# A fused attention and two-expert-layer kernel: the first two dense steps as plain products, sums of token quarters spread over the second, another order of loads and of the last routed block

## Chip, cores and metric

One core of a Trainium2 chip runs the whole kernel in one launch. The metric is the device time of a run in microseconds (us); lower is better.

## What is computed

Three layers in float32, cut here to what matters:

```
x = attention(rotate(q), rotate(k), v)              # 2 x 8 heads, 576 tokens, 64 wide -> x (1152, 512)
# layer 1: each token goes to one of 8 experts
out[e's tokens] = gate * (relu(x[e's tokens] @ w1[e]) @ w2[e])      # w1 (8,512,1024), w2 (8,1024,512)
# layer 2: all tokens go through all 8 experts, weighted by P
P = exp(x @ w_gate - max); 8 times: P /= row sums; P /= column sums; P *= N / E
out = sum over e of P[:, e:e+1] * (relu(x @ w1[e]) @ w2[e])
```

## The kernel before, in words

The matrix products take float32 operands as a high part (float32r) and a low part, the rest: A·B is A_hi·B_hi + A_hi·B_lo + A_lo·B_hi, three passes. ACT rounds the high part (a copy to float32r), DVE subtracts it to get the low part. TensorE (PE) is the engine that all of this feeds.

**Routed part.** Tokens are sorted into blocks of 128 that belong to one expert; `run_blocks` walks over 14 of them (two more sit in a branch that is taken only if the routing needs them). A block's first product is `block_l1` (line 645), its second `block_l2` (672): 8 pieces k of 128 rows, for each the passes hi·hi, hi·lo, lo·hi, all into one PSUM bank. The second weight matrix comes in two halves, each split into `whi` by ACT (L623) and `wlo` by DVE (L616). `block_out` scales the result on ACT (L685) and scatters it to `yd` in DRAM by an indirect DMA of POOL's queue (L686). Beside the blocks, `next(dense)` (L768) moves the generator `dense_experts` on, which loads and splits the first weights of the dense part (blocks 4 to 12).

**Dense part.** All 1152 tokens go through 8 experts in 32 steps of 256 hidden units (`STEPS`). A step's first product is done in the way of Strassen and Winograd: seven products (`l1`, L1086, 12 matmuls of 288 columns each) of sums of quarters of the tokens with sums of quarters of the weights, where plain multiplication takes eight. Quarters 1 to 4 of the tokens and the sums 5, 6, 7 and 4 lie in `yq`, high and low parts apart (index `YQ`). The weights' sums are made by `prep1` in five parts. A step's second product, nine token tiles of six 512-column matmuls (`l2`, L1138), trails by one step: in the loop over n the tiles are of step n - 1. In the first step ACT copies their results to `acc` (L1142); later DVE adds them (L1144, L1149). The tiles go through two PSUM banks ("o"), which the small matmuls of `sinkhorn` (the rounds that make P) use as well.

**The handover.** `yd` is read back in four quarters of 288 tokens (`g`, 576 KB each, 96 partitions with 3 rows of 512, L973). `turn_quarter` (976) transposes a quarter on PE, after as many idle products (L982) as its second argument says, which keep TensorE busy while the load runs; `split_quarter` (989) makes the high and low parts. The first step is done by `plain` (1092) in four calls of 24 matmuls: two terms a, two halves k, three passes, two column halves q. The second step (n = 1 of the loop) already takes the seven products, and the sums of quarters are made as it goes (`sums`, 1004): a DVE operation over 1152 columns (L1007, L1009, L1011), then a split on ACT (L954) and DVE (L955).

Inside `manual_schedule` the order of the code is the order on PE, DVE, ACT and POOL; SP's DMA queue follows its own waits.

Of the kernel before, what the change touches and what calls it, by code (L numbers as in the profile page):

```python
# [10 lines left out]
F32 = mybir.dt.float32  # L11
# [19 lines left out]
NS = 14  # L31
KD_, KF = DM // 128, F // 128
TQ, QW = 96, 288
# [14 lines left out]
def fused_kernel(ctx, tc, qk, vv, tab, cst, emb, tau, w1a, w2a, wg, w1b, w2b, out):  # L48
# [23 lines left out]
    idx = keep.tile([BLK, 2, NB], U32, name="idx")  # L72
    bei = keep.tile([1, NB + 1], I32, name="bei")

    def fetch(raws, src, n, e, cond=None, only=range(4)):
# [436 lines left out]
    with tc.manual_schedule(engines=ORDERED | {mybir.EngineType.SP}):  # L512
# [4 lines left out]
        for k in range(len(units) + LAG):  # L517
# [6 lines left out]
            if 20 < k < 60 and k % 10 in (7, 8):  # L524

                m, x = divmod(2 * (k // 10 - 2) + k % 10 - 7, 4)
                fetch((raw1, raw2)[m], (w1a, w2a)[m], (128, 256)[m], 0, only=(x,))
            if out_rows is not None:
# [142 lines left out]

    def block_l2(h, w, between=None):
        p = bank("y", 2, "y")
        for k in range(KF):
            if k == KF // 2 and between:
                between()
            kk = slice(k * 128, (k + 1) * 128)
            wk = [w[k // 2][x][:, (k % 2) * 512:(k % 2 + 1) * 512] for x in range(2)]
            for n, (a, b) in enumerate(((h[0], wk[0]), (h[0], wk[1]), (h[1], wk[0]))):
                T.matmul(p, a[:, kk], b, start=(k == 0 and n == 0), stop=(k == KF - 1 and n == 2))  # L680
        return p
# [13 lines left out]
    def run_blocks(lo, hi, xb=None, w1=None, w2=None):  # L695
# [11 lines left out]
        with tc.manual_schedule(engines=ORDERED):  # L707
# [10 lines left out]
            for i in range(lo, hi + 1):  # L718
# [32 lines left out]
                if i > lo:  # L751

                    turned = []
                    y = block_l2(h, w2, (lambda: turned.append(block_turn(hn))) if i == hi - 1 else None)
                if i == 1:
# [6 lines left out]
                if here:  # L762
# [3 lines left out]
                    h = turned[0] if i == hi - 1 else block_turn(hn)  # L766
                if NS - 10 <= i < NS - 1:
                    next(dense)  # L768

    reg = [0]  # L770
    with tc.manual_schedule(engines=ORDERED | {mybir.EngineType.SP}):
# [15 lines left out]
        banks(mctx, "pm")  # L787
        dense = dense_experts(ctx, tc, yd, wg, w1b, w2b, out, ident, ones)
        run_blocks(0, NS, xb, pieces(first_w1), first_w2)
# [8 lines left out]

def dense_experts(ctx, tc, yd, wg, w1b, w2b, out, ident, ones):

# [71 lines left out]

    def prep_first():

        for f in range(2):
            yield
            w1[0, f] = wtile(4)
            wsplit(w1[0, f], raw1[0][:, :, f])
        fetch1(2)

# [39 lines left out]
    yield  # L920
    yield from prep_first()
    for part in (0, 1, 1.5, 2, 3):
        yield
        prep1(1, part)
    yield
# [35 lines left out]
    G.memset(wgt, 0.0)  # L961
    nc.sync.dma_start(out=wgt[:, :, :E], in_=wg.rearrange("(k p) e -> p k e", p=128))

# [39 lines left out]

    def sums(p):

# [4 lines left out]
        elif p == 4:  # L1010
            V.tensor_tensor(b21, b21, b22, op=ALU.subtract)  # L1011
        split_sum(p, {5: t1, 6: b22, 7: b11, 4: b21}[p])

# [77 lines left out]

    def plain(r, c):

        d = take()
        w = w1[0, r]
# [3 lines left out]
        for i, (a, y, k, wx, yx) in enumerate(todo):  # L1099
            for q in range(2):  # L1100
                T.matmul(d[1][:, q, :QW], wv[:, wx, a, k], yq[yx][:, y, k, q * QW:(q + 1) * QW],  # L1101
# [51 lines left out]
    with tc.manual_schedule(engines=ORDERED):  # L1153

        hs[0] = htile()
        d = [turn_quarter(0, 40), turn_quarter(1, 0)]
        split_quarter(0, d[0])
        d.append(turn_quarter(2, 6))
        split_quarter(1, d[1])
        c11 = plain(0, 0)  # L1160
        split_quarter(2, d[2])
        d.append(turn_quarter(3, 0))
        c21 = plain(1, 0)
        parts(0, 11, c11)
# [3 lines left out]
        next(sk)  # L1168
        c12 = plain(0, 1)
        parts(0, 21, c21)  # L1170
        sums(6)
        for n in range(2):
            fetch2(n)
        c22 = plain(1, 1)
        parts(0, 12, c12)
        sums(5)
        prep2(0)
        parts(0, 22, c22)
        for n in range(1, STEPS + 1):
            second, last = n == 1, n == STEPS  # L1180

# [24 lines left out]
            do(parts, n, 11)  # L1206
            if second:
                sums(7)
            weights(0)
# [4 lines left out]
            product(5)  # L1214
            if second:
                sums(4)
            tile_(3)
# [75 lines left out]
```

## Time and profile before

| | |
|---|---|
| Runs | 1173.98, 1176.97, 1178.61 us; median 1176.97 |
| The profiled execution | 1175.93 us, span on the core 1174.1 us |
| PE busy | 1134.9 us, 97% of the span |
| DVE, ACT, POOL busy | 833.1, 510.0, 135.0 us |
| Dense matmuls L1086 | 2604 of 288 columns, 381.1 us |
| Dense matmuls L1138 | 1728 of 512 columns, 434.3 us |

Times in the profile count from the span's start. Attention comes first, the routed blocks run to 381 us, the handover to 399.5 us, and the dense steps from there to the end. "Idle before" names what released an engine. Matmuls are pipelined, so their rows overlap and their spacing is shorter than their length.

### The profile page before, as it was taken

The numbers are of one execution on the slowest core, as the hardware profiler recorded it, in microseconds if no ns is written. First come the engines' busy times: TensorE is split into PE (matmuls) and PEld (weight loads), VectorE is DVE, ScalarE is ACT, GpSimd is POOL, SyncE is SP. The second block draws the span as 40 slices with busy tenths as digits, with TensorE's granted clock in tenths as the row PEclk, the third lists the DMA queues.
The fourth block names the chain that finished last, engine by engine and source line by source line (L and its number), as shares of the span: only waits on it lengthen the run. The fifth ranks groups of instructions, "written<-read, shape, count | busy, mean of one in ns | idle before, by whom it ended". The sixth has DMA issues, their size and how long they took to land.

```text
span 1174.1 us, 17220 instructions
## 1 busy us (share of the span) xinstructions
PE 1134.9 (97%) x6698; PEld 970.9 (83%) x6700; DVE 833.1 (71%) x1284; ACT 510.0 (43%) x775; POOL 135.0 (11%) x95
## 2 busy tenths in 40 slices
PE   8798997999999979999999999999999999999998
PEld 3576775788887768999989998999899999989997
DVE  6876766988996368776766676667666766676665
ACT  3555654788986343333333333233323332333230
POOL 4646402134231000000000000000000000000000
PEclk9999998999999999999999999999999999999999
DMA  7478623347285501111111111111111111111002
GB/s 231 115 222 238 181 59 111 127 150 254 69 299 207 127 19 55 54 36 37 54 54 37 36 54 55 37 36 55 53 39 36 54 50 42 37 51 48 29 1 80
DMA packets 74882, 103.63 MB, mean 88 GB/s; under 512 B 5288, under 2 KB 45224, under 8 KB 73904
## 3 DMA queue, kind: packets, MB, share of 16 engines
q1 hardware_dynamic: 71792, 93.54, 26.3%
q0 software_dynamic: 2432, 7.93, 1.9%
q8 instruction: 53, 0.87, 0.3%
q10 hardware_dynamic: 576, 1.05, 0.2%
q14 instruction: 29, 0.24, 0.1%
HBM read 111.09 MB, written 8.39 MB: 102 GB/s over the span
## 4 chain that ended last, share of the span: by engine, by line
PE 63%; DVE 2%; DMA 1%; issue 1%; ACT 1%; SPq 0%; POOLq 0%; ACTq 0%
PE o L1138 33%; PE d L1086 28%; DMA g<-yd 1%; PE d L1101 1%; DMA yd<-y,idx 0%; DVE yq L955 0%; PE o L1030 0%; PE d L985 0%; DVE w L853 0%; DVE h L1126 0%; PE d L982 0%; ACT yq L954 0%; DVE w L915 0%; ACT h L1125 0%; DVE yt L1007 0%
## 5 line engine op out<-in xcount | busy, mean ns | idle before, releaser
L1138 PE MATMUL o<-w,h 128*128 128x512 f32 x1728 | 434.3, 393 | 4.8 <-ACT acc L1142 4.2
L1086 PEld LDWEIGHTS d<-yq,w 128*128 128x128 f32 x2604 | 368.3, 188 | 18.8
L1086 PE MATMUL d<-yq,w 128*128 128x288 f32 x2604 | 381.1, 295 | 0.0
L1138 PEld LDWEIGHTS o<-w,h 128*128 128x128 f32 x1728 | 312.6, 188 | 60.5 <-ACT acc L1142 5.1
L1149 DVE SCALAR_TENSOR_TENSOR acc<-o,P,acc 128x512 f32<-128x512 f32 x252 | 189.2, 751 | 159.6 <-PE o L1138 159.6
L1125 ACT ACTIVATE h<-st 128x576 fp32r<-128x576 f32 x93 | 63.7, 685 | 218.6 <-DVE st L1115 218.5
L1112 ACT ACTIVATE st<-d 128x576 f32<-128x576 f32 x93 | 60.8, 653 | 220.0 <-PE d L1086 220.0
L616 DVE TENSOR_TENSOR wlo<-raw,whi 128x2048 fp32r<-128x2048 f32 x56 | 127.9, 2289 | 14.0 <-ACT whi L623 14.0
L623 ACT ACTIVATE whi<-raw 128x2048 fp32r<-128x2048 f32 x52 | 99.9, 1920 | 8.8 <-DVE n L116 4.0
L1115 DVE TENSOR_TENSOR st<-st,d 128x576 f32<-128x576 f32 x93 | 69.9, 751 | 40.7 <-PE d L1086 40.7
L235 DVE TENSOR_REDUCE nb<-s 120x1 f32<-120x576 f32 (+1 forms) x80 | 60.2, 753 | 36.7 <-PE s L229 26.4
L241 ACT ACTIVATE p<-s,nb 120x576 f32<-120x576 f32 (+1 forms) x80 | 59.1, 738 | 58.2 <-DVE nb L235 56.6
L852 ACT ACTIVATE w<-raw 128x512 fp32r<-128x512 f32 x126 | 72.3, 574 | 19.9 <-DVE raw L898 15.3
L853 DVE TENSOR_TENSOR w<-raw,w 128x512 fp32r<-128x512 f32 x126 | 77.9, 619 | 0.1
L1126 DVE SCALAR_TENSOR_TENSOR h<-st,h 128x576 fp32r<-128x576 f32 x93 | 69.8, 751 | 2.5 <-ACT h L1125 2.4
L229 PE MATMUL s<-kd,qd 128*120 128x288 f32 x280 | 55.7, 322 | 6.0 <-DMA qd<-hl 3.1
L229 PEld LDWEIGHTS s<-kd,qd 128*120 128x120 f32 x280 | 39.5, 183 | 19.6 <-issue 8.2
L282 PE MATMUL o<-ph,vr 120*64 120x288 f32 x320 | 48.1, 421 | 0.0
L680 PE MATMUL y<-wlo,hh 128*128 128x512 f32 x112 | 43.8, 391 | 1.8 <-DVE wlo L616 1.8
L680 PE MATMUL y<-whi,hh 128*128 128x512 f32 x112 | 45.0, 402 | 0.0
L269 DVE COPY ph<-pt 120x480 f32<-120x480 f32 x64 | 41.3, 647 | 2.0 <-PE pt L263 1.7
L686 POOL DMA_INDIRECT yd<-y,idx x14 | 26.5, 1893 | 126.6 <-ACT y L685 96.6
(256 smaller groups left out, 1142.0 us busy)
## 6 DMA issues: line engine op xcount, KB each, us to landing
raw<-w1a SPq DMA_DIRECT2D x56, 512.0 KB
raw<-w2a SPq DMA_DIRECT2D x56, 512.0 KB
raw<-w1b SPq DMA_DIRECT2D x64, 256.0 KB
raw<-w2b SPq DMA_DIRECT2D x32, 512.0 KB
r<-qk SPq DMA_DIRECT2D x7, 1152.0 KB
kd<-hl SPq DMA_DIRECT2D x28, 288.0 KB
qd<-hl SPq DMA_DIRECT2D x24, 144.0 KB
g<-yd SPq DMA_DIRECT2D x4, 576.0 KB
```

Of the source, the lines that this page charges most:

```text
L229: T.matmul(s[:m, h, :HS], qd[:, j, t * QT:t * QT + m], kd[:, j, x, h * HS:(h + 1) * HS], start=(x == 0), stop=(x == 1))
L616: V.tensor_tensor(lo, raw, hi, op=ALU.subtract)
L623: A.activation(hi, raw, AF.Copy)
L680: T.matmul(p, a[:, kk], b, start=(k == 0 and n == 0), stop=(k == KF - 1 and n == 2))
L852: A.activation(hi, src, Copy)
L853: V.tensor_tensor(lo, src, hi, op=ALU.subtract)
L1086: T.matmul(d[1][:, q, :QW], wv[:, wx, which, k], yq[yx][:, YQ[p], k, q * QW:(q + 1) * QW], start=new and k == 0 and (wx, yx) == (0, 0), st ...
L1115: V.tensor_tensor(halves(st[x]), halves(st[x]), mid(d), op=ALU.add)
L1125: A.activation(hi, src, AF.Relu)
L1126: V.scalar_tensor_tensor(lo, src, 0.0, hi, op0=ALU.max, op1=ALU.subtract)
L1138: T.matmul(d, hs[n][:, r, hx, t * 128:(t + 1) * 128], w2[n][:, wx, r], start=(r == 0 and (hx, wx) == (0, 0)), stop=(r == 1 and hx == 1))
L1149: V.scalar_tensor_tensor(a, d, p, a, op0=ALU.mult, op1=ALU.add)
```

## The change

- `block_l2` gets an order for the last block alone (`high_first`): in each half of the pieces the passes with the weights' high part come first, eight of them, and the four with the low part behind. In the order of code this is block 13's second product; blocks 0 to 12 keep theirs.
- The dense weights of steps 0 and 1 are both prepared plain (`prep_plain`): two splits each, without sums. The generator has six stages in place of nine and starts at block 7 in place of 4.
- The gate weights `wg` are loaded during attention (after unit 72) into a small tile `wgk`, and POOL copies them to `wgt`; the load between the first two quarter loads goes.
- A quarter's load puts tokens 3p, 3p+1, 3p+2 into partition p, one piece of 1536 elements; the transposes then write each third column of the bank.
- Idle products: 34 ahead of the first quarter, 6 ahead of the second, none ahead of the third (before: 40, 0, 6).
- Step 1 is done by `plain` as well, in four calls of 24 matmuls. Between them stand the tiles of step 0, the rounds of `sinkhorn` (two for each of the last three calls), and the sums: `split_sums` of one sum, then `add_up` of the next, which is split one call later. The loop begins at n = 2.

```
-    def block_l2(h, w, between=None):
+    def block_l2(h, w, between=None, high_first=False):
...
+        todo = [(k, a, b) for k in range(KF) for a, b in ((0, 0), (0, 1), (1, 0))]
+        if high_first:
+            todo.sort(key=lambda x: (x[0] // (KF // 2), x[2]))
...
-                if NS - 10 <= i < NS - 1:
+                if NS - 7 <= i < NS - 1:
                     next(dense)
...
-    yield from prep_first()
-    for part in (0, 1, 1.5, 2, 3):
-        yield
-        prep1(1, part)
+    for n in range(2):
+        yield from prep_plain(n)
...
-    nc.sync.dma_start(out=wgt[:, :, :E], in_=wg.rearrange("(k p) e -> p k e", p=128))
+    G.tensor_copy(wgt[:, :, :E], wgk)
...
-        nc.sync.dma_start(out=g, in_=yd[i * QW:(i + 1) * QW].rearrange("(t p) d -> p t d", p=TQ))
+        nc.sync.dma_start(out=g, in_=yd[i * QW:(i + 1) * QW].rearrange("(p t) d -> p t d", t=3))
...
-                T.transpose(bank(d[k // 2], k % 2)[:, t * TQ:(t + 1) * TQ], gs[i][:, t, k * 128:(k + 1) * 128],
+                T.transpose(bank(d[k // 2], k % 2)[:, t:QW:3], gs[i][:, t, k * 128:(k + 1) * 128],
...
-        d = [turn_quarter(0, 40), turn_quarter(1, 0)]
+        d = [turn_quarter(0, 34), turn_quarter(1, 6)]
         split_quarter(0, d[0])
-        d.append(turn_quarter(2, 6))
+        d.append(turn_quarter(2, 0))
...
+        c = plain(1, 0, 0, between(0, 0))
         parts(0, 22, c22)
-        for n in range(1, STEPS + 1):
+        split_sums(5)
+        add_up(6)
+        l2(0, 1)
+        parts(1, 11, c)
+        c = plain(1, 1, 0, between(2, 1))
+        split_sums(6)
+        add_up(7)
+        l2(0, 3)
+        parts(1, 21, c)
+        prep1(2, 0)
+        c = plain(1, 0, 1, between(4, 2))
+        split_sums(7)
+        add_up(4)
+        l2(0, 5)
+        prep2(1)
+        parts(1, 12, c)
+        prep1(2, 1)
+        prep1(2, 1.5)
+        c = plain(1, 1, 1, between(6, 3))
+        prep1(2, 2)
+        l2(0, 7)
+        parts(1, 22, c)
+        split_sums(4)
+        prep1(2, 3)
+        l2(0, 8)
+        for n in range(2, STEPS + 1):
```

How the order moves at three places. First PE at the handover (`d` and `o` are PSUM banks, `w` the first dense weights, `io` the identity, `g` the token quarters). Before:

```order
L982 MATMUL d<-w 128x512 x40
L985 MATMUL d<-io,g 128x96 x18
L985 MATMUL o<-io,g 128x96 x6
L982 MATMUL d<-w 128x512 x6
L985 MATMUL d<-io,g 128x96 x12
L1101 MATMUL d<-yq_4045,w 128x288 x2
```

and now:

```order
L985 MATMUL d<-w 128x512 x34
L988 MATMUL d<-io,g 128x96 x12
L985 MATMUL d<-w 128x512 x6
L988 MATMUL d<-io,g 128x96 x6
L988 MATMUL o<-io,g 128x96 x6
L988 MATMUL d<-io,g 128x96 x12
L1108 MATMUL d<-yq_4037,w 128x288 x2
```

The six idle products moved from behind the second quarter's transposes to ahead of them. Second, SP's queue at the same place, before:

```order
L80 DMA raw_77<-w2a 128x2x512
L790 UNCONDITIONAL_BRANCH x2
L973 DMA g<-yd 96x3x512
L962 DMA lw<-wg 128x4x8
L973 DMA g<-yd 96x3x512 x3
L871 DMA raw_4308<-w2b 128x2x512
```

and now:

```order
L81 DMA raw_78<-w2a 128x2x512
L795 UNCONDITIONAL_BRANCH x2
L976 DMA g<-yd 96x1536 x4
L876 DMA raw_4291<-w2b 128x2x512
L876 DMA raw_4293<-w2b 128x2x512
```

The load of `wg` is gone from between the first and the second quarter. Third, DVE in the second dense step (`yt` holds the sums, `yq` their parts, `h` the hidden units' low part), before:

```order
L1115 TENSOR_TENSOR st<-st,d 128x576
L1126 SCALAR_TENSOR_TENSOR h<-st,h 128x576
L1009 TENSOR_TENSOR yt<-yt 128x1152
L955 TENSOR_TENSOR yq_4046<-yt,yq_4045 128x1152
L853 TENSOR_TENSOR w<-raw_3097,w 128x512
L891 TENSOR_TENSOR raw_3097<-raw_3097 128x2x128
```

and now:

```order
L958 TENSOR_TENSOR yq_4038<-yt,yq_4037 128x1152
L1012 TENSOR_TENSOR yt<-yt 128x1152
L1133 SCALAR_TENSOR_TENSOR h<-d,h 128x576
L858 TENSOR_TENSOR w<-raw_3444,w 128x512
L896 TENSOR_TENSOR raw_3444<-raw_3444 128x2x128
L958 TENSOR_TENSOR yq_4038<-yt,yq_4037 128x1152
L1014 TENSOR_TENSOR yt<-yt 128x1152
```

Before, a sum (`yt<-yt`) was split at once (`yq<-yt`); now a split is followed by the next sum, and three other operations stand between that and its split.

## Rows read from the trace of the kernel before

**Rows 1.** Page, part 1: busy time of each engine, share of the span, instructions.
```profile
PE 1134.9 (97%) x6698; PEld 970.9 (83%) x6700; DVE 833.1 (71%) x1284; ACT 510.0 (43%) x775; POOL 135.0 (11%) x95
```

**Rows 2.** Stages: length, busy us of PE, PEld, DVE, ACT, POOL, clock, DMA share, GB/s.
```profile
290.00:373.00 83.00, 83.00 (x407) 69.27 (x406) 74.13 (x57) 69.97 (x66) 24.31 (x12) 1.00 0.57 203
373.00:382.00 9.00, 6.50 (x27) 4.54 (x25) 4.59 (x2) 3.48 (x4) 1.92 (x1) 1.00 0.08 33
382.00:399.50 17.50, 15.56 (x82) 12.80 (x83) 4.30 (x8) 4.22 (x9) 1.18 (x2) 0.90 0.77 176
399.50:416.20 16.70, 16.70 (x163) 15.66 (x162) 8.69 (x13) 8.00 (x15) 0.00 (x0) 1.00 0.11 38
416.20:449.10 32.90, 26.78 (x152) 22.82 (x151) 24.12 (x56) 15.81 (x26) 0.00 (x0) 1.00 0.11 34
449.10:474.60 25.50, 24.89 (x149) 22.26 (x148) 22.27 (x61) 8.27 (x14) 0.00 (x0) 1.00 0.19 57
474.60:498.20 23.60, 23.60 (x139) 21.28 (x139) 15.81 (x26) 7.71 (x12) 0.00 (x0) 1.00 0.17 50
```

**Rows 3.** Timeline of the last routed block: start us, length us, engine, line, op.
```profile
373.44 2.29 DVE L616 TENSOR_TENSOR wlo<-raw,whi 128x2048 fp32r<-128x2048 f32 x1 [1.01 <-ACT whi L623]
...
373.48 0.47 PE L680 MATMUL y<-whi,hh 128*128 128x512 f32 x1
...
375.78 0.50 PE L680 MATMUL y<-wlo,hh 128*128 128x512 f32 x1 [1.83 <-DVE wlo L616]
...
376.21 2.29 DVE L616 TENSOR_TENSOR wlo<-raw,whi 128x2048 fp32r<-128x2048 f32 x1 [0.48 <-ACT whi L623]
...
378.63 0.42 PE L680 MATMUL y<-wlo,hh 128*128 128x512 f32 x1
...
380.94 0.39 PE L680 MATMUL y<-whi,hl__3720 128*128 128x512 f32 x1
381.42 0.69 ACT L685 ACTIVATE y<-y,gate 128x512 f32<-128x512 f32 x1 [5.25 <-issue]
```

**Rows 4.** Timeline of the handover, same columns.
```profile
382.21 9.37 PE L982 MATMUL d<-w 128*128 128x512 f32 x40 [0.89 <-ACTq L790]
382.38 0.97 POOL L686 DMA_INDIRECT yd<-y,idx  x1 [5.81 <-ACTq L790]
...
386.39 0.34 SPq L973 DMA_DIRECT2D g<-yd  x1
386.84 0.40 SPq L962 DMA_DIRECT2D lw<-wg  x1
```

**Rows 5.** PE in the timeline, turning of the token quarters.
```profile
391.61 1.21 PE L985 MATMUL d<-io,g 96*128 96x96 f32 x12
394.52 0.71 PE L985 MATMUL d<-io,g 96*128 96x96 f32 x6 [1.71 <-DMA g<-yd]
...
395.51 2.63 PE L982 MATMUL d<-w 128*128 128x512 f32 x6
397.94 1.79 PE L985 MATMUL d<-io,g 96*128 96x96 f32 x12
399.52 3.42 PE L1101 MATMUL d<-yq,w 128*128 128x288 f32 x24
```

**Rows 6.** One stretch of that turning, columns as in rows 2.
```profile
396.50:397.50 1.00, 1.00 (x3) 0.72 (x3) 1.00 (x4) 0.68 (x2) 0.00 (x0) 0.50 1.06 229
```

**Rows 7.** DMA rate in slices of 0.15 us, from 392 us, then from 398 us.
```profile
GB/s 232 232 218 314 218 218 232 219 219 246 218 232 232 232 232 218 218 232 218 232 314 232 205 232 219 232 246 232 218 218 218 246 218 218 218 218 218 328 232 218
...
GB/s 219 219 287 232 232 328 273 382 314 437 410 382 341 396 423 369 396 341 423 341 246 82 14 0 0 0 0 0 0 0 0 0 0 0 0 109 0 0 0 0
```

**Rows 8.** Waits in the second dense step: us in total, times, longest.
```profile
PE o L1138 <- ACT acc L1142: 4.2, 3, 2.2
ACT yq L954 <- DVE yt L1011: 3.1, 1, 3.1
...
PE o L1045 <- DVE mx L1042: 1.7, 1, 1.7
```

More of the change, by code (lines that the diff above doesn't have):

```diff
@@ L73, in fused_kernel @@
     bei = keep.tile([1, NB + 1], I32, name="bei")
+    wgk = keep.tile([128, KD_, E], F32, name="wgk")
     def fetch(raws, src, n, e, cond=None, only=range(4)):
@@ L527, in fused_kernel @@
                 fetch((raw1, raw2)[m], (w1a, w2a)[m], (128, 256)[m], 0, only=(x,))
+            if k == 72:
+                nc.sync.dma_start(out=wgk, in_=wg.rearrange("(k p) e -> p k e", p=128))
             if out_rows is not None:
@@ L670, in block_turn @@
         return hh, hl_
-    def block_l2(h, w, between=None):
+    def block_l2(h, w, between=None, high_first=False):
         p = bank("y", 2, "y")
-        for k in range(KF):
-            if k == KF // 2 and between:
+        todo = [(k, a, b) for k in range(KF) for a, b in ((0, 0), (0, 1), (1, 0))]
+        if high_first:
+            todo.sort(key=lambda x: (x[0] // (KF // 2), x[2]))
+        for n, (k, a, b) in enumerate(todo):
+            if n == len(todo) // 2 and between:
                 between()
[L677 to L680, printed above, removed]
+            T.matmul(p, h[a][:, k * 128:(k + 1) * 128], w[k // 2][b][:, (k % 2) * 512:(k % 2 + 1) * 512],
+                     start=(n == 0), stop=(n == len(todo) - 1))
         return p
@@ L787, in fused_kernel @@
         banks(mctx, "pm")
-        dense = dense_experts(ctx, tc, yd, wg, w1b, w2b, out, ident, ones)
+        dense = dense_experts(ctx, tc, yd, wgk, w1b, w2b, out, ident, ones)
         run_blocks(0, NS, xb, pieces(first_w1), first_w2)
@@ L796, in fused_kernel, with dense_experts @@
         pass
-def dense_experts(ctx, tc, yd, wg, w1b, w2b, out, ident, ones):
+def dense_experts(ctx, tc, yd, wgk, w1b, w2b, out, ident, ones):
     nc = tc.nc
@@ L871, in fetch2, with prep_plain @@
             nc.sync.dma_start(out=r, in_=w2b[e].rearrange("(r u p) c -> u p r c", r=2, p=128)[c])
-    def prep_first():
+    def prep_plain(n):
         for f in range(2):
             yield
-            w1[0, f] = wtile(4)
-            wsplit(w1[0, f], raw1[0][:, :, f])
-        fetch1(2)
+            w1[n, f] = wtile(4)
+            wsplit(w1[n, f], raw1[n][:, :, f])
+        fetch1(n + 2)
     def prep1(n, part):
@@ L1002, in split_quarter, with add_up @@
             give(x)
-    def sums(p):
+    def add_up(p):
         if p == 6:
@@ L1011, in sums, with split_sums @@
             V.tensor_tensor(b21, b21, b22, op=ALU.subtract)
+    def split_sums(p):
         split_sum(p, {5: t1, 6: b22, 7: b11, 4: b21}[p])
@@ L1090, in l1, with plain @@
         w["left"] -= 1
-    def plain(r, c):
+    def plain(n, r, c, between=None):
         d = take()
-        w = w1[0, r]
+        w = w1[n, r]
         wv = w["t"].rearrange("p x (a k c) -> p x a k c", a=2, k=2)
@@ L1099, in plain @@
         for i, (a, y, k, wx, yx) in enumerate(todo):
+            if i and i % 3 == 0 and between:
+                between(i)
             for q in range(2):
@@ L1155, in dense_experts @@
         hs[0] = htile()
-        d = [turn_quarter(0, 40), turn_quarter(1, 0)]
+        d = [turn_quarter(0, 34), turn_quarter(1, 6)]
         split_quarter(0, d[0])
-        d.append(turn_quarter(2, 6))
+        d.append(turn_quarter(2, 0))
         split_quarter(1, d[1])
-        c11 = plain(0, 0)
+        c11 = plain(0, 0, 0)
         split_quarter(2, d[2])
         d.append(turn_quarter(3, 0))
-        c21 = plain(1, 0)
+        c21 = plain(0, 1, 0)
         parts(0, 11, c11)
@@ L1168, in dense_experts, with between, do @@
         next(sk)
-        c12 = plain(0, 1)
+        c12 = plain(0, 0, 1)
         parts(0, 21, c21)
-        sums(6)
         for n in range(2):
             fetch2(n)
-        c22 = plain(1, 1)
+        c22 = plain(0, 1, 1)
+        prep2(0)
         parts(0, 12, c12)
-        sums(5)
-        prep2(0)
-        parts(0, 22, c22)
-        for n in range(1, STEPS + 1):
-            second, last = n == 1, n == STEPS
+        next(sk)
+        hs[1] = htile()
+        def between(tile, part):
+            def do(i):
+                if i == 6:
+                    l2(0, tile)
+                elif part > 0:
+                    next(sk, None)
+            return do
+        c = plain(1, 0, 0, between(0, 0))
+        parts(0, 22, c22)
+        split_sums(5)
[24 more added lines that the diff above has]
+        for n in range(2, STEPS + 1):
+            last = n == STEPS
             def product(p):
@@ L1206, in dense_experts @@
             do(parts, n, 11)
-            if second:
-                sums(7)
             weights(0)
@@ L1214, in dense_experts @@
             product(5)
-            if second:
-                sums(4)
             tile_(3)
```

2 lines of the change are left out of this document (1 added, 1 removed).

## Prediction

> **What bounds the kernel now.** Start with the page: PE is busy for 97% of the span [rows 1]. Such a share is a mean over stages, so the next view is the table by stage [rows 2]. In the last stretch of routed blocks PE is busy 83.00 of 83.00 us and in the fourth dense step 23.60 of 23.60; a change there must take matmuls away to win anything. Three stages have gaps: the last routed block (6.50 busy of 9.00), the handover (15.56 of 17.50) and the second dense step (26.78 of 32.90, where a step without gaps takes 23.60). All that this change moves lies in or beside these three. So I read three more views: the timeline of the last block [rows 3], that of the handover [rows 4, 5] with its clock and its DMA rate [rows 6, 7], and the waits of the second step [rows 8].
>
> The sum is made against the profiled execution, 1175.93 us, of which 1174.1 is the span; the runs shown have their median 1.0 above it, within their own spread of 4.6.
>
> **Last block, high parts first.** PE starts the product at 373.48, when the first half's high part is there, and then stands 1.83 us, because the second matmul wants the low part that DVE makes from 373.44 on for 2.29 us. The second half's low part takes until 376.21 + 2.29 = 378.50, and its first user runs at 378.63; ten more matmuls follow, 0.23 us apart, the last at 380.94 [rows 3]. In the new order eight matmuls run from 373.48 without any low part, to about 375.3, the four low ones from 375.78, and eight more high ones to about 378.5. The second low part is then again what ends the wait, at 378.63, but only three matmuls follow its first user and not ten: 7 x 0.23 = **1.6 us** earlier. DVE's and ACT's work ahead of it is not touched by more than a split that is 256 columns wider in block 12, and PE had work then [rows 2].
>
> **Dense preparation in the routed blocks.** Five preparation parts become two splits and start three blocks later. ACT and DVE are 70 and 74 of 83 us busy there, but PE never stands [rows 2], so I count 0. The load of the gate weights moves into attention, where one more issue costs some 0.40 us, as it does now [rows 4], of a queue that PE does not wait on: 0. POOL's copy of it has 20 us until its reader: 0.
>
> **Handover.** The idle products and the scatter follow the last block's result [rows 3, 4], so the first quarter's load, issued at 386.39 when the scatter has landed, moves with them: the first transposes go from 391.61 to 390.0. The 34 idle products take 34/40 of 9.37, that is 8.0 us, from 380.6 to 388.6, and end before the data: they no longer bound anything, and 1.4 us of PE stands empty there.
>
> The second quarter came 2.9 us after the first (394.52 against 391.61) [rows 5], and the gate weights' load lay between them [rows 4]. Without it a quarter costs what the DMA rate makes of 576 KB (590 kB): about 225 GB/s, 2.6 us [rows 7]. So the second quarter is there at 392.6 and the third at 395.2. On PE: transposes 390.0 to 391.2, six idle products (1.4 us by the rate of the 40) to 392.6, the second quarter's transposes to 393.9, a wait for the third quarter until 395.2, its 1.2 us, and the first plain product at 396.4. It was at 399.52 before: **3.1 us** earlier, of which 1.6 are the last block's. Part of this comes from the clock: before, the six idle products stood behind the second quarter and took 2.63 us and the third's transposes 1.79 instead of 1.21, because the granted clock was 0.50 there, the 1.2 GHz level, after a stretch of waits and transposes [rows 5, 6]. Now the idle products stand ahead of the second quarter.
>
> Does a row of 6 KB load faster than three of 2 KB? The nearest rows: the quarters, 2 KB pieces into 96 partitions, ran at some 225 GB/s, and the second weights' loads right behind them, also in 2 KB pieces but into 128 partitions, at 340 to 440 [rows 7]. The piece is the same and the rate is not, so the number of partitions seems to decide, and the change leaves that at 96. I take 225 and keep 380 as the other end. The Trainium skill, SBUF — State Buffer, "Door 1: The DMA port swizzle", says the same by a cause: bandwidth depends on how many of 16 ports the partitions reach, and 96 fill half of the ports only half as much. By it the longer row gives nothing.
>
> **Second step, plain.** It takes 32.9 us now, 9.3 more than the fourth step's 23.6 [rows 2]. In this sum: 12 matmuls more at 3.42/24 us [rows 5], +1.7. The small sinkhorn products make the third step 1.9 longer than the fourth; the second step will hold about half as many rounds as now, 1.2 by estimate. The waits: PE stood for 4.2 us in front of tiles of the last product because ACT had not yet copied a tile out of the bank, and ACT stood for 3.1 behind a sum that DVE had not finished [rows 8]. The sum and its split were put next to each other in a queue that also frees the banks. In the new order a sum is split one plain call later (24 matmuls, 3.4 us, and a tile or two), against 1.35 us of DVE for a sum, so ACT should find it ready. PE's 1.7 in front of the maximum's transpose goes too: the maximum now has a whole plain call. I leave 1.0 of waits, since sinkhorn's products still share the two banks. New length 23.6 + 1.7 + 1.2 + 1.0 = 27.5, a gain of 5.4. The sinkhorn rounds that are not done here are done in the third and fourth step, where PE has no gaps: two of them, 0.4 back. **5.0 us**. The low end is that the waits all stay (6.1 idle in place of 1.0): then this part is worth -0.1. The high end, no waits, is 6.0.
>
> **Transposes into each third column** have no row in the trace: 12 take 1.21 us into adjoining columns [rows 5]. Below, nothing; above, a multiple. I take no change, as the nearest row, and price the multiple below.
>
> **Sum:** 3.1 + 5.0 = 8.1 us, 1175.9 - 8.1 = **1167.8 us**, 0.7% faster. About 0.5% (5.9 us) is what a measurement of this kernel can tell from no change; the line lies at 1171.1.
>
> **Rivals.**
> 1. *The longer rows do load at the rate of the second weights.* 590 kB at 380 GB/s is 1.55 us; the third quarter is there at 393.1, then PE's own chain bounds: 390.0 + 1.2 + 1.4 + 1.3 + 1.2 = 395.1, 1.3 more, and some 0.5 from the first quarter: 1166.0. Against it: the piece did not matter between the two loads of rows 7. Chance 0.14.
> 2. *The low clock comes back, later.* There are still waits and transposes from 388.6 to 396.4, and if the 1.2 GHz level falls on the first plain product, it costs again what it cost before: 2.63 - 1.4 for the idle products and 1.79 - 1.21 for the transposes, 1.8 [rows 5]: 1169.6. For it: it happened before in a like stretch [rows 6]. Against it: six idle products now stand in the middle. Chance 0.14.
> 3. *The second step keeps its waits*, with another cause: two PSUM banks for nine tiles and sinkhorn, ACT now without a gap. Then 5.1 comes back: 1172.9, inside 0.5%. Chance 0.12.
> 4. *The other side: strided writes into PSUM slow the transposes.* With x us for each, the first plain product starts at 390.0 + 1.4 + 36x and the fourth quarter, between two plain products, adds 12(x - 0.1). Against 399.5 and the 5.0 of the second step the change breaks even at 48x = 14.3, x = 0.30, three times today's 0.10. At double, 1171.2; at five times 48 x 0.5 - 14.3 = 9.7 slower, 1185.6. Against it: 96 columns in 0.10 us leave TensorE far from one column a cycle at 2.4 GHz, so the writes may have room. Chance 0.10, 0.04 of it at more than three times.
>
> The rule that speaks for the last one stands in the Trainium skill, SBUF — State Buffer, in the same section: PSUM has lines of 8 bytes, and "any non-contiguous PSUM access pattern significantly slows down matmuls". No run here shows it yet and it gives no price; by it the time would lie between 1171 and 1186.
>
> **How the numbers follow.** The forecast holds 0.50. Faster by over 0.5%: forecast, rivals 1 and 2, and a quarter of rival 3, 0.82 with a little of rival 4. Within 0.5%: the rest of 3 and the milder half of 4, 0.14. Slower: 0.04. The range reaches from rival 1 with no waits left in the second step (1166.0 - 1.0, and the spread of the runs, 1163.5) to rival 3 (1172.5); outside lie the dear part of rival 4 and some of rival 3.
>
> **What would show it.** The last block's product without the 1.83 wait and its last matmul near 379.3; the first transposes near 390.0; the quarters' rate still near 225 GB/s; transposes at 12 in 1.2 us; no granted clock under 1.00 after 396; the second step about 27.5 us long, with ACT's wait on DVE's sums gone. A transposes' row of twice the length, or more than 4 us of waits of PE on ACT in the second step, would make the prediction wrong.

## Result and profile after

| | us, median | lowest to highest | runs |
|---|---|---|---|
| before | 1177.24 | 1173.98 to 1178.61 | 4 |
| after | 1165.18 | 1162.47 to 1166.86 | 4 |

The ratio is 0.9902, with a 95% interval of 0.9873 to 0.9931: faster by about 1%, or 12 us. The profiled execution took 1166.86 us, 1165.0 of it the span, 9.1 less than the span of before. It was the slowest of its four, at a mean granted clock of 0.988 where the others had 0.990 and 0.991, so that 9.1 is less than the medians' 12. The forecast was 1167.8, in a range of 1163.5 to 1172.5.

The stages of the changed kernel, as in [rows 2], each with the same work as there (length, busy us of PE, PEld, DVE, ACT, POOL, clock, DMA share, GB/s):

```profile
290.00:373.00 83.00, 82.86 (x406) 69.01 (x405) 71.53 (x51) 69.21 (x63) 24.33 (x11) 1.00 0.63 215
373.00:380.30 7.30, 6.38 (x27) 4.33 (x25) 4.58 (x2) 3.34 (x4) 1.92 (x1) 1.00 0.15 49
380.30:396.20 15.90, 13.31 (x77) 10.81 (x77) 4.30 (x8) 4.46 (x9) 1.39 (x3) 0.97 0.76 184
396.20:414.00 17.80, 17.80 (x162) 16.76 (x161) 7.80 (x12) 6.43 (x13) 0.00 (x0) 0.93 0.20 72
414.00:440.50 26.50, 26.50 (x160) 23.82 (x159) 17.95 (x35) 13.80 (x23) 0.00 (x0) 1.00 0.07 22
440.50:466.20 25.70, 25.34 (x149) 22.55 (x148) 23.87 (x67) 8.71 (x15) 0.00 (x0) 1.00 0.18 55
466.20:490.20 24.00, 24.00 (x144) 21.69 (x143) 19.00 (x40) 8.40 (x13) 0.00 (x0) 1.00 0.17 51
```

The second step is the great change: 26.50 us with PE busy in all of them, where it was 32.90 with 26.78 busy. PE is busy for about as long as before and no longer stands. The last block is shorter by 1.7. The handover is shorter by 1.6, but the first plain step behind it is 1.1 longer, at a mean clock of 0.93.

The last routed block in the timeline, to hold against [rows 3] (start us, length us, engine, line, operation):

```profile
373.26 2.29 DVE L619 TENSOR_TENSOR wlo<-raw,whi 128x2048 fp32r<-128x2048 f32 x1 [1.01 <-ACT whi L626]
...
373.31 0.47 PE L684 MATMUL y<-whi,hh 128*128 128x512 f32 x1
...
375.61 1.21 PE L684 MATMUL y<-wlo,hh 128*128 128x512 f32 x4 [0.22 <-DVE wlo L619]
...
378.51 1.09 PE L684 MATMUL y<-wlo,hh 128*128 128x512 f32 x4
```

PE's wait for the first low part is 0.22 us in place of 1.83, and only four matmuls stand behind the second one, which DVE still finishes at 376.04 + 2.29 = 378.33.

PE's rows of the handover, and SP's issue of the four quarter loads, to hold against [rows 4, 5]:

```profile
380.49 1.19 PE L985 MATMUL d<-w 128*128 128x512 f32 x4 [0.89 <-ACTq L795]
382.64 7.00 PE L985 MATMUL d<-w 128*128 128x512 f32 x30 [0.96 <-issue]
389.55 1.21 PE L988 MATMUL d<-io,g 96*128 96x96 f32 x12
390.54 1.62 PE L985 MATMUL d<-w 128*128 128x512 f32 x6
392.12 0.71 PE L988 MATMUL d<-io,g 96*128 96x96 f32 x6
...
394.77 1.72 PE L988 MATMUL d<-io,g 96*128 96x96 f32 x12 [1.44 <-DMA g<-yd]
396.20 4.52 PE L1108 MATMUL d<-yq,w 128*128 128x288 f32 x24
...
383.52 2.74 SPq L976 DMA_DIRECT2D g<-yd  x4
```

The 34 idle products come in two parts, with 0.96 us between them in which PE waited for nothing that the profile shows, and end at 389.64, as the transposes begin. The first quarter's 12 transposes take 1.21 us, as before [rows 5], though they now write every third column. The third quarter makes PE wait for 1.44 us; its transposes take 1.72 and the first plain product 4.52 instead of 3.42. That is the clock, by a window over them:

```profile
395.30:398.50 3.20, 3.20 (x17) 3.20 (x16) 2.52 (x5) 1.80 (x3) 0.00 (x0) 0.50 0.88 286
```

A granted clock of 0.50 is the 1.2 GHz level. It fell during the transposes behind the wait; before, it had fallen in a like place, ahead of the first plain product [rows 6].

The waits of the second step (us in total, times, longest; the list has no row of PE any more, compare [rows 8]):

```profile
ACT acc L1149 <- PE o L1145: 13.2, 8, 6.1
...
```

ACT now waits for PE, 13.2 us in all, and its 3.1 us behind DVE's sum are gone.

**Where the 9.1 us of the span came from.** The last block's first matmul stands 0.17 earlier. From there to its last matmul it is 1.57 less. From that to the start of the fourth plain product 0.48 less, from there to the first tile of the sixth step 5.81 less, and from there to the end 1.08 less. The last was not foreseen: it is 28 steps of 23.513 us instead of 23.553.

### The profile page after: what moved, and what is told of

Same layout as the page of the kernel before. It is cut to its first block, busy times and chain, and to the rows that moved or that the text cites. A ratio compares the mean times of both kernels' runs of the same rounds, so it can differ in the third digit from the quotient of the medians.

```text
span 1165.0 us, 17223 instructions
## 1 busy us (share of the span) xinstructions
PE 1134.7 (97%) x6706; PEld 970.5 (83%) x6706; DVE 828.4 (71%) x1275; ACT 507.1 (44%) x770; POOL 135.9 (12%) x96
## 3 DMA queue, kind: packets, MB, share of 16 engines
q1 hardware_dynamic: 71024, 93.54, 26.5%
## 4 chain that ended last, share of the span: by engine, by line
PE 64%; DVE 1%; DMA 1%; issue 0%; SPq 0%; POOLq 0%
PE o L1145 34%; PE d L1091 28%; PE d L1108 2%; DMA g<-yd 1%; DMA yd<-y,idx 0%; DVE acc L1151 0%; PE o L1035 0%; PE d L988 0%; DVE h L1133 0%; DVE w L858 0%; SPq L976 0%; DVE w L920 0%; DVE acc L1156 0%; DVE P L1070 0%; DVE rs L1059 0%
## 5 line engine op out<-in xcount | busy, mean ns | idle before, releaser
L1091 PEld LDWEIGHTS d<-yq,w 128*128 128x128 f32 x2520 | 355.1, 188 | 18.6
L1091 PE MATMUL d<-yq,w 128*128 128x288 f32 x2520 | 366.7, 294 | 0.0
L1133 DVE SCALAR_TENSOR_TENSOR h<-st,h 128x576 fp32r<-128x576 f32 x90 | 67.4, 749 | 0.4 <-ACT h L1132 0.3
L1133 DVE SCALAR_TENSOR_TENSOR h<-d,h 128x576 fp32r<-128x576 f32 x38 | 28.8, 757 | 20.4 <-ACT h L1132 20.4
```

What stands on the lines that cost most here:

```text
L1091: T.matmul(d[1][:, q, :QW], wv[:, wx, which, k], yq[yx][:, YQ[p], k, q * QW:(q + 1) * QW], start=new and k == 0 and (wx, yx) == (0, 0), st ...
L1133: V.scalar_tensor_tensor(lo, src, 0.0, hi, op0=ALU.max, op1=ALU.subtract)
```

## Experiments

The place where the routed blocks begin differs between runs by up to 7 us (196.7 to 204.0), from attention, where the edits add one small load at most. So single totals are of little use, and the runs are compared by stretch. The columns: the last block from its first matmul to its last; from that to the first matmul of the fourth plain product (the handover and most of the first step), with the length of granted clock 0.50 in it; from there to the first tile of the sixth step (all that happens in the second step, and what is given back later); and one steady step, a mean over 24.

| kernel | last block | to 4th plain | low clock there | to sixth step | steady step |
|---|---|---|---|---|---|
| before | 7.46 | 32.14 | 3.4 | 110.28 | 23.553 |
| after | 5.89 | 31.66 | 3.4 | 104.47 | 23.513 |
| after, again | 5.88 | 30.05 | none | 104.47 | 23.513 |
| high parts first alone | 5.90 | 30.69 | none | 110.23 | 23.553 |
| plain second step alone | 7.46 | 34.08 | 6.8 | 104.58 | 23.553 |
| all but plain second step | 5.87 | 29.48 | none | 114.12 | 23.513 |
| sums together | 5.88 | 31.34 | 3.4 | 109.66 | 23.513 |
| rows of 2 KB | 5.87 | 29.46 | none | 104.46 | 23.513 |
| same bytes, 128 partitions | 5.90 | 28.78 | none | 104.48 | 23.513 |
| idle products in the gap | 5.90 | 29.30 | none | 104.48 | 23.513 |
| full width | 5.87 | 32.05 | none | 104.46 | 23.513 |
| gate load put back | 5.88 | 29.64 | none | 104.61 | 23.553 |
| gate load back, tile kept | 5.88 | 29.57 | none | 104.48 | 23.513 |
| second tile | 5.89 | 29.55 | none | 104.57 | 23.553 |

### The parts one by one

**High parts first alone**, in the kernel before:

```diff
-    y = block_l2(h, w2, (lambda: turned.append(block_turn(hn))) if i == hi - 1 else None)
+    y = block_l2(h, w2, (lambda: turned.append(block_turn(hn))) if i == hi - 1 else None, i == hi)
```

> The kernel before with the new order of the last block's second product alone. My theory: the product's last matmul starts 1.6 us earlier against its first one (5.9 us after it, not 7.5), and all that follows moves with it, the first transposes by 1.6 to 2.0 us; the second dense step keeps its 32.9 us. Rival: the scatter and the load of the first quarter end on something else (the scatter before, a queue), and the first transposes do not move although the product ends earlier.

Measured: 1172.94 us in one run. The last block takes 5.90, the whole 1.56 of the change. PE's rows of its handover:

```profile
383.03 8.37 PE L984 MATMUL d<-w 128*128 128x512 f32 x36 [1.10 <-issue]
391.23 1.65 PE L987 MATMUL d<-io,g 96*128 96x96 f32 x18
...
394.15 1.65 PE L984 MATMUL d<-w 128*128 128x512 f32 x6 [0.78 <-ACT yt L834]
395.64 1.15 PE L987 MATMUL d<-io,g 96*128 96x96 f32 x12
396.58 1.17 PE L1103 MATMUL d<-yq,w 128*128 128x288 f32 x7
```

The first transposes come at 391.23, 0.38 earlier than before and not 1.6: the 40 idle products run right up to them, so they bound. The first plain product nevertheless starts 2.94 earlier (396.58 against 399.52). The second quarter was there in time, where PE had waited 1.71 us for it [rows 5], and the clock did not fall: from the six idle products to the first plain product it is 2.43 us, where it was 4.01. The second step is as before.

**Plain second step alone**, with the sums spread, and all else as before:

```diff
+        c = plain(1, 0, 0, between(0, 0))
+        split_sums(5)
+        add_up(6)
...
-            if second:
-                sums(7)
```

> The kernel before with the second step plain and its sums spread, nothing else of the change. My theory: the second step falls from 32.9 to 26.5 us, the third and fourth give 0.5 back, PE's waits for ACT's copies (4.2 us) are gone, and the run is about 6 us faster. Rival: the gain of the whole change is in the handover's loads, and the step alone gives under 3 us, because the sums' parts come later relative to the products that read them.

Measured: 1170.54 us (median of 10), ratio 0.9961, 0.9942 to 0.998. Its second step and the stretch ahead of the first plain product, in windows:

```profile
393.00:399.80 6.80, 6.30 (x29) 5.62 (x30) 3.29 (x7) 2.96 (x6) 0.00 (x0) 0.50 1.06 282
417.10:443.20 26.10, 26.10 (x156) 23.57 (x156) 17.98 (x35) 13.84 (x23) 0.00 (x0) 1.00 0.07 21
```

The second step is 26.10 without a gap, counted from its first plain product; in the changed kernel that is 26.02, and the 26.50 above has 0.5 of small products ahead of it in addition. The stretch to the sixth step is 5.7 less than before: this part alone makes all of that gain. The handover had 6.8 us of low clock in this run, twice that of before, and took 1.9 longer.

**All but the plain second step**, as an edit of the changed kernel:

```diff
-        for n in range(2, STEPS + 1):
+        for n in range(1, STEPS + 1):
...
+            if second:
+                sums(7)
```

> The whole change without the plain second step and its sums (the step in seven products as before). My theory: the first plain product of the first step comes about 3 us earlier than before, the second step stays near 32.9 us, and the run is 2 to 4 us faster than before. Rival: the parts need each other, and without the plain step the run is either no faster at all or as fast as the whole change.

Measured: 1174.58 us (median of 10), ratio 0.9965, 0.9942 to 0.9989. The handover kept all it could win (first plain product at 395.67, 3.85 earlier). The second step lost it again: it took 36.8 us, not the 32.9 that were expected. Its window, and a part of it:

```profile
412.40:449.20 36.80, 30.67 (x152) 25.92 (x151) 24.28 (x56) 15.73 (x26) 0.00 (x0) 0.86 0.12 40
...
433.10:443.30 10.20, 8.70 (x26) 7.04 (x26) 7.31 (x16) 4.53 (x8) 0.00 (x0) 0.50 0.16 51
```

Its waits are those of [rows 8]:

```profile
PE o L1143 <- ACT acc L1147: 4.2, 3, 2.2
...
ACT yq L959 <- DVE yt L1016: 3.1, 1, 3.1
```

In this run the clock fell among these waits, for 10.2 us, and the stretch to the sixth step took 3.8 us longer than before. Six of its ten executions had a mean granted clock of 0.984 or 0.985 like this one, and took 1174.3 to 1176.9 us; the other four had 0.988 to 0.993 and took 1165.6 to 1172.6. So the waits cost more than their own time: they are a place where the clock can fall, which the plain step takes away.

**Sums together:** the plain second step, but three of the four sums added right ahead of their splits, as before:

```diff
         split_sums(5)
-        add_up(6)
         l2(0, 1)
...
+        add_up(6)
         split_sums(6)
```

> The changed kernel with each sum of quarters computed right ahead of its split and not one plain call earlier. My theory, that the spread takes ACT's wait for DVE's sum away: ACT stands 1.3 us or more at each of three splits, tiles' copies queue behind it, PE waits for the bank, and the second step grows by 1 to 4 us from 26.5. Rival: the plain calls alone took the waits away, because PE has more to do between tiles, and the second step stays within 0.3 us.

Measured: 1168.79 us in one run. Windows over the second step and two stretches behind it:

```profile
411.00:437.80 26.80, 26.56 (x157) 23.48 (x157) 16.52 (x33) 13.47 (x22) 0.00 (x0) 1.00 0.06 21
437.80:442.80 5.00, 2.17 (x16) 2.03 (x15) 3.77 (x5) 2.30 (x4) 0.00 (x0) 1.00 0.00 0
442.80:446.20 3.40, 3.40 (x11) 2.86 (x10) 2.88 (x11) 0.19 (x1) 0.00 (x0) 0.50 0.51 143
```

The second step itself hardly suffers: 26.77 from its first plain product to the next step's first product, where the changed kernel has 26.02. The third does: PE stands 2.83 us in front of a tile, as its row says, and then runs at the low clock.

```profile
442.50 2.71 PE L1145 MATMUL o<-w,h 128*128 128x512 f32 x6 [2.83 <-ACT acc L1149]
```

In all 5.2 us are lost (109.66 against 104.47): 0.75 in the second step, 2.83 in that wait, and the rest in the low clock and smaller waits behind it. Plain products without the spreading keep 0.6 of the 5.8 us that both together win. Some 1.6 of the loss are the low clock, which need not fall each time; without it they would keep 2.2. So in these runs **the spread of the sums earns most of the gain**, by one run without it. Spreading them without plain products wasn't tried. The delay shows up a step later than its cause: the sums stand in the second step, and it is in the third that PE waits for a bank which ACT has not copied out.

### The loads of the quarters

**Rows of 2 KB:** three pieces for a partition, and adjoining columns:

```diff
-        nc.sync.dma_start(out=g, in_=yd[i * QW:(i + 1) * QW].rearrange("(p t) d -> p t d", t=3))
+        nc.sync.dma_start(out=g, in_=yd[i * QW:(i + 1) * QW].rearrange("(t p) d -> p t d", p=TQ))
...
-                T.transpose(bank(d[k // 2], k % 2)[:, t:QW:3], gs[i][:, t, k * 128:(k + 1) * 128],
+                T.transpose(bank(d[k // 2], k % 2)[:, t * TQ:(t + 1) * TQ], gs[i][:, t, k * 128:(k + 1) * 128],
```

> The changed kernel with the quarters loaded as before (token t*96+p in row t of partition p, 2 KB pieces) and adjoining columns in the transposes. My theory: the number of partitions sets the rate, so the quarters still follow each other by 2.5 to 2.7 us, the first plain product starts within 0.4 us of 396.2, and the transposes take 1.2 us for 12 as with every third column. Rival: pieces of 6 KB load faster, and with 2 KB the second and third quarter come at least 1 us later; or adjoining columns make the transposes shorter.

Measured: 1160.42 us in one run (its routed blocks begin 4.4 us earlier than those of the changed kernel). PE's rows:

```profile
385.24 1.16 PE L988 MATMUL d<-io,g 96*128 96x96 f32 x12
...
389.72 1.18 PE L988 MATMUL d<-io,g 96*128 96x96 f32 x12 [0.92 <-ACT yq L952]
390.68 3.43 PE L1108 MATMUL d<-yq,w 128*128 128x288 f32 x24
```

Its transposes take 1.16 to 1.18, the changed kernel's at the same clock 1.18 to 1.21: the stride costs nothing that shows. While the second and third quarters load, the DMA view of 384.1 to 389.6 counts these packets, and that of the changed kernel, from 389.5 to 394.6, those under them:

```profile
DMA packets 672, 1.31 MB, mean 238 GB/s; under 512 B 34, under 2 KB 34, under 8 KB 672
```

```profile
DMA packets 240, 1.17 MB, mean 230 GB/s; under 512 B 32, under 2 KB 32, under 8 KB 240
```

A third of the packets move the bytes at the same rate, a packet three times as large taking three times as long (0.43 us for 6 KB against 0.14 for 2 KB, means of the trace). The longer row gives nothing.

**Same bytes, 128 partitions:** each quarter's load goes into 128 partitions, with pieces of 4.5 KB:

```diff
-g = gt[:TQ, i % 2 * 3 * DM:(i % 2 + 1) * 3 * DM].rearrange("p (t d) -> p t d", t=3)
+g = gt[:, i % 2 * 1152:(i % 2 + 1) * 1152]
...
```

> The changed kernel with each quarter's bytes loaded into 128 partitions, 4.5 KB to each, and not 96 with 6 KB; the transposes read 96 of them and other columns, so the tokens that go into the dense part are not the right ones. My theory, that the number of partitions sets the rate: some 380 GB/s in place of 225, quarters 1.5 to 1.7 us apart in place of 2.6, no wait for the third quarter, and the first plain product 1.5 to 2 us earlier relative to the first load's issue. Rival: it is the source, rows of a tensor that has just been written, or the queue, and the rate stays near 225.

Measured: 1163.29 us in one run. Packets from 387.7 to 392.4, and PE's rows:

```profile
DMA packets 558, 1.80 MB, mean 383 GB/s; under 512 B 46, under 2 KB 46, under 8 KB 558
```

```profile
388.41 1.16 PE L988 MATMUL d<-io,g 96*128 96x96 f32 x12
...
391.82 1.15 PE L988 MATMUL d<-io,g 96*128 96x96 f32 x12
393.70 3.45 PE L1108 MATMUL d<-yq,w 128*128 128x288 f32 x24 [0.73 <-ACT yt L837]
```

383 GB/s in place of 230: **the number of partitions sets the rate**, not the length of the row. A quarter of these bytes belong to the second weights' loads behind, but the quarters alone show the same: the last pieces of the first three land 1.7 and 1.6 us apart, in the changed kernel 2.6. The rule of the Trainium skill, SBUF — State Buffer, "Door 1: The DMA port swizzle", has the direction right; its ports, half of them with all their partitions and half with half of them, would let 96 partitions load at 0.75 of the rate, an estimate of 287 from the 383, and 230 were measured. The third quarter no longer makes PE wait, and the stretch to the fourth plain product is 0.5 to 1.3 us shorter than in the runs with 96 partitions and no low clock.

**Full width**, an attempt to have that with the tokens in their places: two blocks of 128 tokens a quarter, its last 32 tokens in 32 partitions of their own, idle products recut:

```diff
+nc.sync.dma_start(out=gt[:, i * 2 * DM:(i + 1) * 2 * DM].rearrange("p (t d) -> p t d", t=2),
+                  in_=yd[i * QW:i * QW + 256].rearrange("(t p) d -> p t d", p=128))
+nc.sync.dma_start(out=gt[32 * i:32 * i + 32, 8 * DM:9 * DM], in_=yd[i * QW + 256:(i + 1) * QW])
...
+d = [turn_quarter(0, 28), turn_quarter(1, 5)]
...
+d.append(turn_quarter(2, 2))
```

> The changed kernel with each quarter loaded as two blocks of 128 tokens into 128 partitions and its last 32 tokens into 32 partitions of their own, and with the idle products cut anew (28, 5 and 2 instead of 34, 6 and 0). Theory that the number of partitions sets the rate: quarters land some 1.6 to 1.9 us apart instead of 2.5 (590 kB at 380 GB/s is 1.55), no clock falls with the idle products there, and the first plain product starts 9.8 to 10.6 us after the first quarter's load is issued (12.8 in the changed kernel's profile, 11.7 to 11.9 in the runs without a low clock): 1.2 to 2.5 us of the time, about 1163. Theory that the rate is limited elsewhere (the three parts of a quarter, the queue): quarters stay 2.4 us or more apart and the first plain product comes 11.5 us or more after the issue, no gain over the changed kernel.

Measured: 1167.86 us (median of 6), ratio 0.992, 0.9891 to 0.995: no gain over the changed kernel, whose second set of runs on that chip had 0.9902, and a miss for the forecast of 1163. PE's rows:

```profile
390.02 1.87 PE L988 MATMUL d<-io,g 32*128 32x32 f32 x10 [0.40 <-DMA g<-yd]
...
395.77 2.19 PE L988 MATMUL d<-io,g 128*128 128x128 f32 x12
397.88 3.44 PE L1108 MATMUL d<-yq,w 128*128 128x288 f32 x24
```

Behind the first quarter no transpose waited for a load, but 12 of them now take 2.19 us where 12 of 96 rows took 1.2. Three of the four quarters are turned ahead of the first plain product, so 3 x 1.0 us lie on the path, more than the loads gave. The starts in the trace tell which are the dear ones. Two transposes of 128 rows stand 0.11 us apart at the head of a group, before any of 32 rows. Behind that, one of 32 rows comes 0.20 us after one of 128, the next of 128 rows 0.17 after that, and the second of 128 again 0.17: 0.54 for three, where three of 96 rows take 0.25. So the price comes with the 32-row transposes among the others, which also hold up those behind them.

### The load of the gate weights, and 0.04 us a step

**Gate load put back** into the handover, its early tile gone:

```diff
-    wgk = keep.tile([128, KD_, E], F32, name="wgk")
...
-    G.tensor_copy(wgt[:, :, :E], wgk)
+    nc.sync.dma_start(out=wgt[:, :, :E], in_=wg.rearrange("(k p) e -> p k e", p=128))
```

> The changed kernel with the gate weights' load back between the first and second quarter's load. My theory: 512 pieces of 32 bytes hold the queue for some 0.3 to 0.5 us, so the second quarter, the third and the first plain product come that much later. Rival: the small pieces also slow the first quarter or cost several us, so that moving them away is most of what the handover won; or nothing at all, since the loads overlap.

Measured: 1169.5 us in one run. The handover is as short as without it (29.64 us to the fourth plain product, and 29.57 in the next run): the load between the quarters cost nothing that shows, where the prediction had counted it into the 2.9 us between the first two quarters. But the steady step is 23.553 again.

**Gate load back, tile kept**, an unused tile of the same 128 bytes a partition in its place:

```diff
+    pad = keep.tile([128, KD_, E], F32, name="pad")
```

> The changed kernel with the gate weights loaded in the handover as before, but with an unused tile of the same size as the gate weights' early one where that one stood, so that all later tiles keep the addresses they have in the changed kernel. Theory that the place of the tiles in SBUF sets the length of a steady dense step: 23.513 us, as in the changed kernel, though the load is back. Theory that the early load itself does it: 23.553 us, as before and as in the run with the load put back and no such tile.

Measured: 1163.02 us in one run. Two starts of the same matmul, 24 steps apart, in two windows of the timeline:

```profile
535.01 0.62 PE L1144 MATMUL o<-w,h 128*128 128x512 f32 x2
...
1099.33 0.62 PE L1144 MATMUL o<-w,h 128*128 128x512 f32 x2
```

564.32 / 24 = 23.513. So it is not the load but the tile. By the order of allocation it moves every later one by 128 bytes; the trace has no addresses.

**Second tile:** the changed kernel with another 128 bytes:

```diff
     wgk = keep.tile([128, KD_, E], F32, name="wgk")
+    pad = keep.tile([128, KD_, E], F32, name="pad")
```

> The changed kernel with a second unused tile of 128 bytes a partition behind the gate weights' early one, so that every later tile stands 256 bytes further on than in the kernel before, 128 further than in the changed kernel. If the steady dense step depends on where a tile falls within a line of 256 bytes, it goes back to 23.553 us; if it gets shorter with each shift, 23.47; if one end of a buffer was in the way and is now out of it, 23.513 stays. The second dense step, 26.0 us without a low clock, should not move by more than 0.1.

Measured: 1171.07 us in one run, and the same two starts:

```profile
540.73 0.63 PE L1147 MATMUL o<-w,h 128*128 128x512 f32 x2
...
1106.00 0.63 PE L1147 MATMUL o<-w,h 128*128 128x512 f32 x2
```

565.27 / 24 = 23.553: back. At shifts of 0 (four profiles) and 256 bytes (one) a step takes 23.553, at 128 (nine) it takes 23.513, whatever else differs. What in the chip makes it so is open. By the starts of a step's nine tiles, eight of the nine intervals are 3 to 8 ns shorter and one is 12 ns longer.

### The low clock in the handover

**Idle products in the gap:** five more, in front of the third quarter's transposes:

```diff
-        d.append(turn_quarter(2, 0))
+        d.append(turn_quarter(2, 5))
```

> The changed kernel with five idle products in the gap ahead of the third quarter's transposes. My theory: TensorE keeps its granted clock at 1.00, the transposes take 1.2 and not 1.7 us, the first plain product 3.4 and not 4.5, and the second plain product starts 1.0 to 1.6 us earlier. Rival: the fall to 1.2 GHz comes from the time before 392 us and happens again, so that the five products only fill the gap, 0 gained.

Measured: 1162.66 us in one run.

```profile
390.59 1.39 PE L985 MATMUL d<-w 128*128 128x512 f32 x5
392.10 1.21 PE L988 MATMUL d<-io,g 96*128 96x96 f32 x12
393.10 3.41 PE L1108 MATMUL d<-yq,w 128*128 128x288 f32 x24
```

The wait of 1.44 is filled, and the transposes and the product run at a granted clock of 1.00.

**After, again:** the changed kernel once more.

> The changed kernel itself once more, on one chip with the others. If the low clock in the handover is chance, this profile may show the first plain product at 11.7 to 11.9 us after the first quarter's load instead of 12.8; if the edit brings it, a stretch of granted clock 0.5 of some 3 us starts again within 2 us of the third quarter's transposes. The second step should take 26.0 us when no low clock lies ahead of it and a steady step 23.513 us either way.

Measured: 1164.26 us (median of 6, 1160.42 to 1167.88), ratio 0.9902, 0.9872 to 0.9931. The first plain product came 12.2 us after the first load's issue, 12.7 in the first profile. This time a wait as long had no such effect:

```profile
392.07 1.18 PE L988 MATMUL d<-io,g 96*128 96x96 f32 x12 [1.35 <-DMA g<-yd]
393.04 3.42 PE L1108 MATMUL d<-yq,w 128*128 128x288 f32 x24
```

The low clock is thus not tied to the kernel: of the eleven profiles with the new handover it fell in two, of the three with the old one in two. In one kernel, with and without it, the stretch took 31.66 and 30.05: it costs 1.6 us, 0.5 of them on the third quarter's transposes and 1.1 on the first plain product. That the idle products in the gap prevent it is not shown by one run, since most runs without them went well too. Beyond the clock they win nothing that these runs can tell: 29.30 stands beside 29.5 to 30.05, and the first transposes alone start anywhere from 4.9 to 6.3 us after the first load's issue. No version was shown to be faster than the changed kernel.

## Why the prediction came out

**The last block:** right, 1.57 for 1.6, and by the mechanism named: the second low part still ends the wait, with fewer matmuls behind it.

**The handover:** right in kind, and the size depended on the clock. The first transposes came at 389.55 (390.0 forecast) and the first plain product at 396.20 (396.4). That these fit is in part luck. The first load was issued 2.9 us earlier than before (383.52 against 386.39 [rows 4]) and not 1.6, but its last piece took 6.0 us to land, where it had taken 5.2. The 34 idle products took 9.15 us and not 8.0, because of the 0.96 us in which PE stood behind the fourth; such a stand, of 0.6 to 1.3 us, is in eleven of the fourteen profiles and not in that of before, and its cause is open. So the step that they "no longer bound anything" is not borne out. In nine of the eleven profiles with the new handover the transposes start as the idle products end, and in the run with rows of 2 KB the chain that ends with the first plain product goes through them (view of the chain from 374 to 392; start, length, what):

```profile
377.28 1.13 issue
378.40 6.99 PE d L985 x30
385.40 0.99 PE d L988 x12
```

Fewer of them, with the loads as they are, were not tried.

Behind the start of the first plain product 1.1 us went back, since the clock fell: the second rival, at a chance of 0.14 and a price of 1.8, in this run. With the 0.5 that it took from the transposes ahead, it cost 1.6. The step that failed in this run is that six idle products in the middle would hold the clock up. They end ahead of the second quarter, and the wait of 1.44 for the third comes behind them. Why the clock held behind the same wait in most other runs is open. In the repeated run the clock held, and the stretch from the last block's last matmul to the fourth plain product was 2.1 us shorter than before. Of the loads and the recut together the runs without a low clock show 0.6 to 1.2 us (30.69 in the one run with the old handover, 29.5 to 30.05 with the new).

**The gate load** between the quarters was taken as part of the 2.9 us between them. Put back, it costs nothing that shows. The term, 0.3 us of the sum (2.6 for 2.9), was wrong; it did not show in the total.

**The rows of 6 KB:** right, no gain, 230 GB/s where 225 were taken, and 128 partitions take 383, so the first rival falls for the reason given.

**The strided transposes:** right, no cost: 1.18 to 1.21 for 12 against 1.16 to 1.18. The fourth rival, and with it the sentence of the Trainium skill, SBUF — State Buffer, "Door 1: The DMA port swizzle", on non-contiguous PSUM access, does not hold for these transposes; where page and trace differ, the trace decides.

**The second step:** the mechanism right, its size a little short: 26.5 for 27.5. The mis-sized term is the 1.0 us of waits left over, which were none. The third and fourth step gave back 0.6 for the 0.4 forecast, so that the part is worth 5.8 and not 5.0. The third rival fell. In the run with the sums together waits cost 5.2 us, close to the 5.1 that the rival was given; but most of them came in the third step, set off by the sums, and a low clock was among them, so the likeness is chance.

**The rest:** the prediction had nothing there, and 1.1 us came from 28 steps at 0.04. With it the sum of the profile reads 0.2 + 1.6 + 0.5 + 5.8 + 1.1 = 9.1 for the 8.1 forecast. Against the sum, the handover beside the last block gave 1.0 less (0.5 for 1.5), the second step 0.8 more, the steady steps 1.1 and the part ahead of the last block 0.2 more: the total fits better than its parts, which is luck. By the medians the gain is 12 us, 4 more than forecast; the executions differ in their clock, and how much of the 4 that makes was not measured.

## What to carry to other kernels

- A wait in a queue that also frees buffers is paid for where the buffers are wanted, here a step later. Put the operation that makes an operand a whole product ahead of the one that uses it, and look at the step behind the edit too.
- Waits of TensorE cost their own time and, in some runs, the clock of what follows them. Compare kernels stretch by stretch, with the granted clock beside each, before an edit gets the credit or the blame for it.
- For loads into SBUF count the partitions before the length of the rows, but price what the other layout does to the operations that read it.

## What the runs showed that was not expected

A tile of 128 bytes a partition, used or not, makes each steady step 0.04 us shorter, and two such tiles do not. The edit's real use of it, the early load of the gate weights, showed no gain. And the clock among the old waits of the second step fell for 10 us in one of the three profiles that have them and not at all in the two others, which alone is 3.8 us.
